# Attention and feed-forward in one kernel: the last 64 rows of unseparated projections as a pair, the output weights in two transfers, and a new timetable

## The chip, the cores and the metric

The kernel runs on one core of a Trainium2 chip. The metric is the time of one execution on the device in microseconds (us), the median of several runs. The engines are TensorE (PE in the profile; PEld is its loading of weights), VectorE (DVE), ScalarE (ACT), GpSimd (POOL) and SyncE (SP), which here does nothing but issue transfers. TensorE writes its results to eight banks of PSUM, from which VectorE and ScalarE read.

## The reference

One layer of a transformer on 2048 tokens of width 576, all in bf16:

```python
# attention, 32 heads of 18, four segments of 512 tokens
q, k, v = (layernorm(x) @ w for w in (wq, wk, wv))          # per head
for s in range(4):
    p = softmax(q_s @ k_s.T * scale + causal_mask)
    a_dot = p @ v_s
    a_mem = phi(q_s) @ M / (phi(q_s) @ z + 1e-6)            # memory of the segments before
    o_s = g * a_mem + (1 - g) * a_dot                        # g = sigmoid(beta), per head
    M += phi(k_s).T @ v_s;  z += sum(phi(k_s))
h = x + concat(o) @ wo
out = h + gelu(layernorm(h) @ w1 + b1) @ w2 + b2             # 576 -> 4608 -> 576
```

## The kernel before, in words

The work is cut into operations (`Op`) of a few instructions each, some 1,900 of them: for each segment s the stages X (layer norm of x and its transposition), P (projections q, k, v), A (scores, exp, mask, values, memory), M (update of the memory), B (output projection, residual, layer norm), C (first matrix of the feed-forward, `F1`) and D (second matrix, `F2`). A tag and a name make a key: `P1Pk` is the first half of the k projection in stage P of segment 1, `P1Rk` its second half, and the index after it is the tile of 128 tokens.

**The order is written out.** `TIMETABLE` gives every operation a rank and an engine: in `"P1Pk": "p 222 159 318 243"` the four tiles' first halves run on TensorE (p) at ranks 222, 159, 318 and 243; a is ScalarE, d VectorE, g GpSimd, s SyncE. `Graph.schedule` takes the operations by rank, gives out the buffers (`Slots`, `Buf.pick`) and keeps an account of the time with a cost for each operation. Each engine issues its own operations in that order, so one that waits holds up everything behind it on its engine. The account steers which buffer is taken and in which form a projection is made; it does not delay anything on the chip. For a transfer it takes `dma = max(dma, op.end) + op.size / 295e3` and then 1.8 us until the data can be used.

**Projections.** A projection multiplies 128 tokens by a 576 x 576 matrix, in two halves of 288 columns that go to two PSUM banks. The 576 rows of the contraction are laid out as five blocks: four of 128 rows and a last one of 64, which is stored twice, once in partitions 0 to 63 for the first half of the columns and once in 64 to 127 for the second, with zeros elsewhere. `proj_pair` has two ways to make it:

- *separated*: `fn_a` (`P`) runs pairs of 64-row matmuls, the lower rows for one bank, the upper rows for the other, side by side in the array: five pairs; `fn_b` (`R`) makes four more pairs with the banks changed over. Between the two a small memset on VectorE or GpSimd (`pass`) keeps them apart.
- *unseparated* (`fused`): where P and R stand next to each other in TensorE's order, ten full-row matmuls of 128 rows run at R's place (L885) and P and `pass` issue nothing. The last block costs a full matmul for each half although half of its rows are zeros.

TensorE works in one tile mode at a time: 128 rows (full), 64-row pairs (`rows64`: separated projections and F1), four 32-row tiles (`rows32`: scores), four 32-column tiles (`cols32`: values). The account charges `SWITCH["pe"]` for each change of mode.

**Transfers.** Nearly all are issued by SyncE (`load`, L663; `flip`, L670, a transfer that transposes; `qkst`, L951). In the first minute these matter here: the loads of x and of the weights q, k, v; the first load of x is followed by a mark (`gate_x`, L743) that has to be made before the third tile of x and the q weights are issued; `dma` 4 is beta (to 32 gates), 5 the output weights (`wt_o`, 720 KB in one transfer), 6 the bias b1, 7 the bias b2. `A0flip` 0 to 7 turn q and k of segment 0, `X1flip`, `X2flip`, `X3flip` the normalized x of the later segments (`xreg<-xnd`), `A1flip` and so on q and k of the later segments into four score buffers (`qk`).

In the lines of the profile L859 is the pair of 64-row matmuls in `rows`, L885 the full-row matmul of `fn_b`, L898 the plain projections of the first two tiles, L802 a transposition on TensorE, L1067 and L1227 the scores, L1098 and L1252 the values, L1198 and L1201 the memory, L1364 and L1401 F1, L1453 F2, L1016 the exp, L677 to L683 the copies out of PSUM.

## Time and profile before

| | |
|---|---|
| median of three runs | 439.85 us (439.02, 439.85, 442.82) |
| span of the profiled execution | 439.3 us |
| TensorE busy | 431.0 us (98%), 5182 matmuls |
| VectorE, ScalarE, GpSimd busy | 288.5, 298.2, 176.5 us |
| transferred | 75.61 MB, mean 172 GB/s |
| packets of the queues named instruction | 56 (q8: 40, q14: 16) |

The profiled execution's own time is its span, 439.3 us, from the first to the last instruction; the runs' times were taken apart from it and lie between 0.3 us below and 3.5 us above. A row of groups reads: line, engine, operation, out<-in, shapes, count, then busy us and mean ns of one, then the idle time before them and who ended it. In the chain of work each piece begins where the one before it ended, so a change of mode in front of it is part of it. A row of busy time by stretch gives for each engine the busy us and the number of instructions.

### The profile page before, as it was taken

To read this page: it belongs to the slowest core of one execution; us is meant where nothing else is said; L and a number is where in the kernel's file an instruction comes from. 1 tells how busy PE (TensorE), PEld (TensorE's weight loads), DVE (VectorE), ACT (ScalarE), POOL (GpSimd) and SP (SyncE) were. 2 spreads that over 40 slices of the span, in tenths; PEclk is the share of its full clock that TensorE was granted. 3 is DMA by queue.
4 is the path that set the end of the run, shared out by engine and by line. 5 is a ranking of instruction groups with operands and counts; after the bars stand their busy time and mean duration, and the time that the engine had idled before them with its cause. 6 is when DMAs were issued, how large, how long until landed. Compare 5 with 4: busy or idle time off the path is not lost.

```text
span 439.3 us, 12412 instructions
## 1 busy us (share of the span) xinstructions
PE 431.0 (98%) x5182; PEld 279.0 (64%) x5182; DVE 288.5 (66%) x641; ACT 298.2 (68%) x325; POOL 176.5 (40%) x328
## 2 busy tenths in 40 slices
PE   8998999999999999999999999999999999999997
PEld 5665677776677676664445766654457785446886
DVE  5898889988997987975698897766776211000002
ACT  5997988999888897788898976657864003465000
POOL 6676866445867644571631462320203001020001
PEclk9999999999999999999999999999999999999999
DMA  7699999989899758973671859506405752450011
GB/s 229 214 209 230 347 262 273 234 274 229 236 235 340 196 157 231 229 157 101 155 185 26 243 152 213 107 18 213 140 25 143 233 131 81 151 175 1 1 58 51
DMA packets 80280, 75.61 MB, mean 172 GB/s; under 512 B 57952, under 2 KB 67424, under 8 KB 80224
## 3 DMA queue, kind: packets, MB, share of 16 engines
q1 hardware_dynamic: 80080, 74.74, 63.9%
q8 instruction: 40, 0.66, 0.7%
q14 instruction: 16, 0.13, 0.1%
q10 hardware_dynamic: 144, 0.09, 0.1%
HBM read 42.30 MB, written 18.87 MB: 139 GB/s over the span
## 4 chain that ended last, share of the span: by engine, by line
PE 89%; DMA 4%; DVE 3%; SPq 1%; POOL 1%; ACT 1%; issue 1%; DVEq 0%; POOLq 0%
PE bank L1453 33%; PE bank L1364 24%; PE bank L859 9%; PE bank L1401 8%; PE bank L1227 4%; PE bank L885 3%; PE bank L1252 3%; DMA xreg<-xnd 2%; DMA x<-in_A_x_dram 2%; PE bank L1201 1%; PE bank L1098 1%; PE bank L1067 1%; SPq L663 1%; SPq L670 1%; PE bank L1198 1%
## 5 line engine op out<-in xcount | busy, mean ns | idle before, releaser
L1016 ACT ACTIVATE pt<-bank 128x1024 bf16<-128x1024 f32 x160 | 155.5, 1021 | 36.7 <-PE bank L1227 26.5
L1453 PEld LDWEIGHTS <-hT 128*128 128x128 bf16 x1188 | 111.3, 98 | 33.4 <-issue 6.6
L1364 PE MATMUL bank<-xreg,w1g 64*128 64x512 bf16 x972 | 107.7, 377 | 0.0
L1364 PEld LDWEIGHTS <-w1g 64*128 64x128 bf16 x972 | 46.2, 94 | 57.2 <-issue 3.0
L1453 PE MATMUL bank<-w,hT 128*128 128x288 bf16 (+2 forms) x594 | 77.8, 283 | 0.0
L1453 PE MATMUL bank<-w_lo,hT 128*128 128x288 bf16 (+2 forms) x594 | 77.6, 283 | 0.0
L1466 DVE TENSOR_TENSOR ot<-bank,hc 128x288 bf16<-128x288 f32 (+2 forms) x33 | 14.1, 444 | 85.1 <-PE bank L1453 79.6
L1241 POOL TENSOR_SCALAR_AFFINE_SELECT pt<-pt 128x512 bf16<-128x512 bf16 x57 | 38.0, 680 | 45.4 <-ACT pt L1016 45.1
L1369 ACT ACTIVATE hT<-bank,b_col 128x512 bf16<-128x512 f32 x36 | 22.1, 690 | 46.4 <-PE bank L1364 46.3
L1439 POOL TENSOR_TENSOR hc<-hc,b_bc 128x576 f32<-128x576 f32 x11 | 14.5, 1333 | 83.6 <-DMA hc<-hd 83.6
L1379 DVE TENSOR_SCALAR hT<-bank,b_col 128x512 bf16<-128x512 f32 x45 | 32.6, 742 | 19.4 <-PE bank L1364 17.3
L1401 PE MATMUL bank<-xreg,w1g 64*128 64x256 bf16 x648 | 38.4, 270 | 0.0
L1401 PEld LDWEIGHTS <-w1g 64*128 64x128 bf16 x648 | 30.5, 94 | 6.6 <-issue 3.2
L1384 ACT ACTIVATE hT<-hT 128x8192 bf16<-128x8192 bf16 (+2 forms) x6 | 31.8, 5320 | 0.1
L859 PE MATMUL bank<-hT,xreg 64*128 64x288 bf16 x414 | 27.7, 283 | 1.7 <-DMA xreg<-xnd 1.7
L885 PE MATMUL bank<-hT,xreg 128*128 128x288 bf16 x210 | 28.4, 287 | 0.3 <-ACT pt L1016 0.2
L1412 DVE TENSOR_TENSOR hT<-bank,b_col 128x512 bf16<-128x512 f32 x33 | 21.4, 681 | 6.3 <-PE bank L1401 5.9
L1377 ACT ACTIVATE hT<-bank,b_col 128x512 bf16<-128x512 f32 x27 | 17.8, 686 | 11.4 <-PE bank L1364 11.0
L859 PEld LDWEIGHTS <-xreg 64*128 64x128 bf16 x414 | 19.6, 94 | 8.3 <-DMA xreg<-xnd 1.9
L1227 PE MATMUL bank<-qk 32*128 32x512 bf16 (+3 forms) x384 | 24.2, 301 | 0.2 <-DVE hT L1379 0.2
L885 PEld LDWEIGHTS <-xreg 128*128 128x128 bf16 x210 | 19.7, 98 | 6.4 <-issue 1.0
L773 POOL TENSOR_TENSOR ln<-ln,mhalf 128x1 f32<-128x1 f32 x32 | 19.5, 610 | 2.7
(122 smaller groups left out, 566.4 us busy)
## 6 DMA issues: line engine op xcount, KB each, us to landing
w1g<-in_B_w_dram SPq DMA_DIRECT2D x41, 576.0 KB, 4.9
qkd<-qk_pad SPq DMA_DIRECT2D x15, 512.0 KB, 4.7
hd<-h SPq DMA_DIRECT2D x16, 288.0 KB, 4.6
hc<-hd SPq DMA_DIRECT2D x16, 288.0 KB, 4.0
w_lo<-in_B_w_dram SPq DMA_DIRECT2D x3, 864.0 KB, 7.2
w<-in_B_w_dram SPq DMA_DIRECT2D x3, 864.0 KB, 8.4
xb<-in_A_x_dram SPq DMA_DIRECT2D x16, 144.0 KB, 4.7
x2d<-xn SPq DMA_DIRECT2D x14, 160.0 KB, 2.8
```

The source lines that it names most:

```text
L859: return nc.tensor.matmul(out=half(hf), lhsT=xTb.t[r, k, ts], rhs=wt[r, hf, k, :], start=start, stop=stop, skip_group_check=True)
L885: nc.tensor.matmul(out=half(hf), lhsT=xTb.t[:, k, ts], rhs=wt[:, hf, k, :], start=(k == 0), stop=(k == KT - 1))
L1016: ops.append(add(prio, {"act": 1.04}, lambda e, j=j: nc.scalar.activation(out=pt.t[:, 2 * j:2 * j + 2, :], in_=st[j].t[:], func=ACT.Exp, s ...
L1227: nc.tensor.matmul(out=st[i // 2].t[:, i % 2, off:off + n_], lhsT=qk[rows, 1, kt * P:(kt + 1) * P], rhs=qk[rows, 0, kt * P:L], start=True, ...
L1241: nc.gpsimd.affine_select(out=blk, in_=blk, pattern=[[0, 4], [1, P]], compare_op=ALU.is_ge, fill=0.0, base=0, channel_multiplier=-1)
L1364: nc.tensor.matmul(out=cc[w].t[:], lhsT=w1.t[rows, k, q, :], rhs=x2T[s].t[rows, k, :], start=(k == 0), stop=(k == ND - 1))
L1369: ready_f[f + w] = [add(pf - 12, {"act": 0.68}, lambda e, f=f, w=w, cc=cc: nc.scalar.activation(out=hT[:, :, f + w, :], in_=cc[w].t[:].rea ...
L1379: nc.vector.tensor_scalar(out=dst, in0=src, scalar1=b, scalar2=None, op0=ALU.add)
L1384: ge = add(2.9, {"act": 0.42 * (f1 - f0) + 0.2}, lambda e, f0=f0, f1=f1: nc.scalar.activation(out=hT[:, :, f0:f1, :], in_=hT[:, :, f0:f1, ...
L1401: nc.tensor.matmul(out=cc[w].t[:, q * 2 * P:(q + 1) * 2 * P], lhsT=w1.t[rows, k, q, :], rhs=x2T[s].t[rows, k, ts], start=(k == 0), stop=(k ...
L1412: nc.vector.tensor_tensor(out=dst, in0=src, in1=b.unsqueeze(2).to_broadcast([P, 2, 2 * P]), op=ALU.add)
L1453: nc.tensor.matmul(out=c.t[:, 0:c1 - c0], lhsT=hT[:, tl // 2, f, (tl % 2) * P:(tl % 2 + 1) * P], rhs=w2_c[ch][:, f - ch * WCH, c0:c1], sta ...
```

## The change

Three things change in the code, and with them the timetable.

1. An unseparated projection can take one of two new forms. With `first`, the 64 rows of the last block go first, as one pair in the two halves of the array, and then four full-row matmuls for each half of the columns; with `last` the pair comes at the end. The form is chosen in `schedule`, where by its account (`TAILED`, and `SWITCH` for each change of mode) it costs less than the plain one.
2. The output weights come in two transfers of 360 KB, issued at two places.
3. The account of transfers in `schedule` counts TensorE's instructions: for each `FETCH` matmuls a fetch of `LAG` us is added to a second clock of the transfers, and a transfer ends with the later of the two clocks plus `LAND`. The sizes and costs that the account uses for many transfers and a few operations are changed (qkst from 560e3 to 342e3, the flips of x2 from 520e3 and 420e3 to 953e3 and 667e3, the beta load from 8e3 to 250e3, gates from 1.7 to 0.73 us, and so on); these numbers alone issue nothing.
4. `TIMETABLE` is new throughout: nearly every rank changes, and some operations change their engine. The rows that the text below speaks of are shown.

```diff
-SWITCH = dict(act=1.35, pe=0.1)
+SWITCH = dict(act=1.35, pe=0.095)
 FUSED = 1.225
+TAILED = 1.103
...
-    "A00st0": "p 96 115",
+    "A00st0": "p 86 108",
...
-    "A0flip": "s 104 112 120 118 180 193 207 287",
+    "A0flip": "s 127 116 140 146 168 182 198 326",
...
-    "A1flip": "s 449 405 534 607 496 636 667 788",
+    "A1flip": "s 411 409 558 591 466 655 475 770",
...
-    "P1Pk": "p 222 159 318 243",
+    "P1Pk": "p 215 161 306 237",
-    "P1Rk": "p 226 165 322 257",
+    "P1Rk": "p 222 164 313 241",
...
-    "X00dma": "s 22 26 32 14",
+    "X00dma": "s 44 49 51 17",
-    "X1dma": "s 63 72 176 161",
-    "X1flip": "s 198",
+    "X1dma": "s 61 70 176 155",
+    "X1flip": "s 228",
-    "X3flip": "s 490 604",
+    "X3flip": "s 491 593",
-    "b1": "d 313",
-    "dma": "s 1 12 13 39 28 195 144 262",
+    "b1": "a 257",
+    "dma": "s 1 15 16 59 55 256 935",
-    "gate": "g 7",
-    "gates": "a56 d79",
+    "gate": "g 12",
+    "gates": "a66 d67",
-    "memset": "d10 g27 g54 d30 a50 a69 a66 a91 g47 g15 g6",
+    "memset": "d7 g27 g8 d11 a125 a48 a58 a28 g9 g29 g4",
-    "tri": "g 82",
+    "tri": "g 10",
+    "wodma": "s 195 81",
...
+MATMULS = dict(F1=18, F2=6, st=7, st0=13, val=16, mem=3, TX=5, TQ=8, T=5, M=16, warm=4, C00F1=36, C01F1=36, A01val=48)
+MATMULS.update({h + nm: 10 if h == "P" else 8 for h in "PR" for nm in "kqvo"})
+FETCH, LAG, LAND = 128, 0.66, 1.95
...
             if op.fused:
                 c = 0.0 if op.mate is not None else FUSED
-            kind = op.mode if e == "pe" else op.table
+                if op.mate is None:
+                    was, then = table.get("pe"), op.next_mode
+                    s = SWITCH["pe"]
+                    plain = FUSED + s * (was != "full") + s * (then != "full")
+                    first = TAILED + s + s * (was != "rows64") + s * (then != "full")
+                    last = TAILED + s + s * (was != "full") + s * (then != "rows64")
+                    if min(first, last) < plain - 1e-9:
+                        op.form = "first" if first <= last else "last"
+                        c = TAILED + s + s * (was != ("rows64" if op.form == "first" else "full"))
+                        table["pe"] = kind = "full" if op.form == "first" else "rows64"
...
+            issued += op.mm if e == "pe" else 0
+            while issued >= fetched:
+                pending.append(t0)
+                fetched += FETCH
...
             if e == "sp":
+                while pending and pending[0] <= op.end:
+                    slow = max(slow, pending.pop(0)) + LAG
                 dma = max(dma, op.end) + op.size / 295e3
-                op.end = dma + 1.8
+                slow = max(slow, op.end) + op.size / 295e3
+                op.end = max(dma, slow) + LAND
...
+                n = KT if b.form is None else KT - 1
+                if b.form == "first":
+                    for w in range(2):
+                        rows(w, w, KT - 1, True, False)
                 for hf in range(2):
-                    for k in range(KT):
-                        nc.tensor.matmul(out=half(hf), lhsT=xTb.t[:, k, ts], rhs=wt[:, hf, k, :], start=(k == 0), stop=(k == KT - 1))
+                    for k in range(n):
+                        nc.tensor.matmul(out=half(hf), lhsT=xTb.t[:, k, ts], rhs=wt[:, hf, k, :], start=(k == 0 and b.form != "first"),
+                                         stop=(k == n - 1 and b.form != "last"), skip_group_check=True)
+                if b.form == "last":
+                    for w in range(2):
+                        rows(w, w, KT - 1, False, True)
...
-        w_ok["o"] = load_w(4, "o", 3, begin)
+        gr.tag = "wo"
+        w_ok["o"] = [load(4, lambda h=h: wts["o"][:, h, :, :].rearrange("p k d -> p (k d)"),
+                          lambda h=h: A_w[3 * P:4 * P, h * KT * HALF:(h + 1) * KT * HALF], 316e3, [xn_ok[0, 0]]) for h in range(2)]
+        gr.tag = ""
```

With the output weights out of the row `dma`, its index 5 is b1 and 6 is b2 in the new timetable. TensorE's ranks of the steps that the text names, before and after: `A1st` 3 at 582 and 585, `P3Pk` 2 at 634 and 640, `D00hc` 0 at 848 and 936.

66 lines of the change are left out of this document (36 added, 30 removed), and 603 rows, old and new, of the table TIMETABLE.

## The prediction

> **What bounds the kernel now.** I read the page first, then the busy time by stretch, then TensorE's waits.
>
> ```profile
> span 439.3 us, 12412 instructions
> PE 431.0 (98%) x5182; PEld 279.0 (64%) x5182; DVE 288.5 (66%) x641; ACT 298.2 (68%) x325; POOL 176.5 (40%) x328
> ```
> ```profile
> 0.00:60.00 60.00, 54.63 (x820) 38.27 (x822) 50.21 (x129) 50.14 (x71) 42.67 (x109) 1.00 0.92 245
> 60.00:366.00 306.00, 305.79 (x3720) 195.86 (x3715) 232.71 (x500) 225.92 (x219) 130.07 (x217) 1.00 0.69 180
> ```
> ```profile
> PE bank L859 <- DMA xreg<-xnd: 1.7, 1, 1.7
> PE bank L692 <- PEq L1609: 0.8, 1, 0.8
> PE bank L939 <- ACT qk_pad L677: 0.5, 1, 0.5
> PE bank L1098 <- DVE pt L1079: 0.4, 1, 0.4
> PE bank L1067 <- DVE MZacc L996: 0.4, 2, 0.2
> PE bank L802 <- DVE xn L788: 0.3, 1, 0.3
> ...
> PE bank L1227 <- DVE hT L1379: 0.2, 1, 0.2
> ```
>
> TensorE is the bound, at full clock. Its idle time is 5.4 us in the first 60 us (60 less 54.63) and 0.2 us in the next 306. The longest waits (all eleven add up to 5.3 us) sit in the first stretch too, where the 16 DMA engines are 92% busy. The rest of the 8.3 us idle is the tail behind the last matmul, which the change leaves as it is. So the change can win in two ways only: fewer matmuls or mode changes, or waits in the first minute of the timetable. It can lose anywhere, because the timetable of every engine is new.
>
> **Fewer matmul slots, more mode changes.** The counts per projection come from these groups, the price of one from two pieces of the chain that follow different neighbours:
>
> ```profile
> L885 PE MATMUL bank<-hT,xreg 128*128 128x288 bf16 x210 | 28.4, 287 | 0.3 <-ACT pt L1016 0.2
> L859 PE MATMUL bank<-hT,xreg 64*128 64x288 bf16 x414 | 27.7, 283 | 1.7 <-DMA xreg<-xnd 1.7
> L859 PE MATMUL bank<-wt_o,oT 64*128 64x288 bf16 x234 | 15.7, 283 | 0.0
> ...
> L885 PE MATMUL bank<-wt_o,oT 128*128 128x288 bf16 x30 | 4.2, 287 | 0.0
> ```
> ```profile
> 85.43 0.33 PE bank L1227 x8
> 85.76 2.56 PE bank L885 x20
> 88.31 0.33 PE bank L1227 x8
> 88.64 7.82 PE bank L859 x126
> ...
> 97.44 0.32 PE bank L1198
> 97.77 2.45 PE bank L885 x20
> ```
>
> A separated projection is 18 matmuls, an unseparated one 10: (414+234)/18 = 36 and (210+30)/10 = 24, together the 60 of the code. Twenty full-row matmuls take 2.45 us behind a full-row matmul (L1198) and 2.56 behind a 32-row score (L1227): 0.1225 us each, 1.225 an unseparated pass, and about 0.1 for a change of tile mode. The seven separated passes (x126, 63 pairs) take 7.82: less the change, 0.122 a pair, so 1.10 for the nine pairs. A tailed pass has one pair and eight full-row matmuls, 9 x 0.1225 = 1.10.
>
> In the new timetable 34 projections have both halves next to each other. By the rule in the scheduler 30 of them get the tail (17 first, 13 last; each stands beside an operation of another mode) and 4 stay plain. So 20 fewer plain passes: 20 x (1.225 - 1.10) = -2.5 us. Reading TensorE's order in both timetables, mode changes rise from 193 to 222, with the one inside each tail: 29 x 0.10 = +2.9 (2.8 at 0.095, the diff's own figure; 3.2 at 0.11). Net **+0.4 us** (0.2 to 0.8). No cover: TensorE is the bound. Ten fewer separated passes also means ten fewer marks (`pass`) on VectorE and GpSimd; no wait of TensorE on them is listed, so nothing.
>
> **The flip that TensorE waits for.** SyncE issues in order:
>
> ```profile
> 30.20 0.59 SPq L663 DMA_DIRECT2D wt_o<-in_A_w_dram  x1
> 30.90 1.25 SPq L670 DMA_TRANSPOSE xreg<-xnd  x1
> 32.75 0.33 SPq L951 DMA_DIRECT2D qkd<-qk_pad  x1
> 33.13 3.79 SPq L670 DMA_TRANSPOSE w_lo<-qkd  x1
> ```
> ```profile
> 30.90 9.12 DMA xreg<-xnd
> ```
> ```profile
> DMA  1000699999990900000000000090000001909939
> ...
> q14 instruction: 1, 0.01, 3.0%
> q8 instruction: 1, 0.02, 1.7%
> ```
>
> The last view is 36 to 40 us in 40 slices. The flip X1flip lands 9.1 us after its issue, and TensorE, ready at 38.4 (40.07 less 1.67), waits. Ahead of the flip stand the 720 KB of output weights. But from slice 13 to 34 (2.2 us) the engines move almost nothing although four transfers are under way; in that time two instruction packets run, 1.7% and 3.0% of 16 x 4 us, or 1.1 and 1.9 us. So half of this wait belongs to the fetches, which come with the count of instructions, not with the order of the transfers.
>
> The new order sends one half of the output weights ahead (behind the load of x, order 81, where DMA has room) and leaves 360 KB at the old place. But it also puts X1flip behind A0flip6, the transposing load at 33.13, whose issue alone held SyncE 3.79 us. TensorE comes to X1flip's first user, P1Pk3, behind the same work. Lower end: the wait goes, -1.7. Upper end: A0flip6's issue again stands 3.79 us, X1flip is issued at 34.6 and needs 9.1, lands at 43.7: a wait of 5.3, or +3.6. The half that left takes about 2 us off (6.4 against 4.4 below), one more flip puts back 1.3 (its usual issue), and the fetch finds X1flip under way again. I take a wait of 1.5: **-0.2**, nearest the row of the wait itself.
>
> **The start.**
>
> ```profile
> 3.28 0.18 POOL L743 CAST mark<-x 1x1 f32<-1x1 bf16 x1 [1.02 <-DMA x<-in_A_x_dram]
> 11.03 0.23 ACT L1507 ACTIVATE g_bc<-beta_bc 128x32 f32<-128x32 bf16 x1 [1.44 <-DMA beta_bc<-in_A_beta_dram]
> ```
> ```profile
> L659 POOL MEMSET qk_pad<- 128x896 bf16 x2 | 1.7, 842 | 0.0
> ...
> L1490 POOL TENSOR_SCALAR_AFFINE_SELECT tri<-tri 128x128 bf16<-128x128 bf16 x1 | 0.3, 293 | 0.1
> L1489 POOL MEMSET tri<- 128x128 bf16 x1 | 0.2, 204 | 0.0
> ```
>
> - The beta load moves behind the third load of x, so x lands earlier and the wait on VectorE's xn (L802, 0.3) goes: **-0.3**.
> - ScalarE's gates exp waits for beta with the q copy queued behind it; the new order has it behind the copy: -0.4 of the 0.5 us wait at L939. Against this, GpSimd now makes one qk_pad memset (0.84), the gmz column and tri (0.5) ahead of the mark that lets SyncE issue the q weights; it was free 1.02 us before, so the mark comes about 0.4 later, and the q weights are used as they land: +0.4. Together **0** (-0.4 to +0.4).
> - The first scores (A00st0) go ahead of a projection, so exp and mask start about half a microsecond earlier; of the waits on masks and banks (L1098, L1067: 1.1 with the smaller ones) I take a third, **-0.4** (0 to -1.1).
>
> **Other moved transfers.**
>
> ```profile
> hT<-in_A_w_dram SPq DMA_DIRECT2D x4, 360.0 KB, 4.4
> ...
> wt_o<-in_A_w_dram SPq DMA_DIRECT2D x1, 720.0 KB, 6.4
> ...
> b_bc<-in_B_b_dram SPq DMA_DIRECT2D x1, 144.0 KB, 6.4
> ...
> xreg<-xnd SPq DMA_TRANSPOSE x5, 6.4
> ...
> ot<-in_B_b_dram SPq DMA_DIRECT2D x1, 9.0 KB, 3.9
> ```
>
> The b1 load comes later and its copy goes from VectorE to ScalarE: in that queue P1's ek and the exps of A02 stand behind a load that takes 3.9 us; cover is the projections B00 and B01, which need no ScalarE, so 0, and up to +3.9 with the cover gone. The b2 load goes from the first minute to just ahead of its first user, the hc of D00; 6.4 us, covered by D00's own F2 groups and six other banks: 0.
>
> In segment 1, X3flip1 now stands behind A1flip3, which waits for a score buffer that the step A1st3 frees. TensorE has 7.4 us of work from there to the flip's user P3Pk2 (three unseparated passes 3.7, one pair of separated ones 2.2, steps and values 1.5); A1flip3's issue 1.3 and the usual 6.4 of such a flip make 7.7: **+0.3** (0 to +3.0, when it takes 9.1 as above). All other weight loads are issued at the same distance or earlier: 0, as only 0.2 us of waits stood there before.
>
> By the Trainium skill ("DMA: Bandwidth & Descriptors", section "Bandwidth"), larger transfers run nearer the peak; its table (0.95 us for 64 KB, 6.15 for 1 MB) gives, as an estimate, 0.6 us fixed for each. By that the split would cost 0.6 us of queue and the sum would be 440.2; the rows above (360 KB 4.4, 720 KB 6.4) show only that two halves in turn would be dearer, not two that overlap. The same page (section "Queues, rings and completion order") says that each DMA engine takes turns between queue rows packet by packet; then a fetch costs one packet's turn, 1.1 us, not the 2.2 seen, and the sum would be 1.1 lower.
>
> **The sum.** +0.4 -0.2 -0.3 +0 -0.4 +0.3 = -0.2 against the span of 439.3: 439.1. The median of the runs, 439.85, is 0.5 above that span, so **439.6 us**.
>
> **The rivals.**
>
> - *The account is right and the first minute closes up.* X1flip's wait goes (-1.7), TQ's (-0.4), xn's (-0.3), the mask waits (-1.1), against +0.4: -3.1, or 436.7. For it: nothing after 60 us waits. Against it: the fetch at 36 us will come again.
> - *SyncE stands at A0flip6* (the other side). X1flip lands at 43.7: +3.6, with +0.4 and -0.7 of the start +3.3: 443.1. It decides where that issue takes more than about 2.5 us. For it: the row with 3.79. Against it: with 360 KB less queued the issue should come nearer the usual 1.3.
> - *X3flip1 is late by the whole 3.0* behind A1flip3: 442.3. It decides above 6.1 us from issue to landing.
> - *The tails do not pay.* Within the forecast: 2.5 won, 2.9 spent, so the change to tails alone is no gain.
>
> **How the numbers follow.** Forecast 0.55 (own range 438 to 441.3), first minute closed 0.17, SyncE at A0flip6 0.16, X3flip1 0.12. The range 436.8 to 443.3 leaves out about 2 in 10. A measurement of this kernel can tell about 1% from no change, 4.4 us. Faster by that needs nearly all of the 5.3 us of waits gone despite the switches: 0.04, out of the second case. Slower needs one of the last two with more than its price, or both: 0.12. Within: 0.84.
>
> **What the profile would show.** L885 with some 280 matmuls (30 x 8 + 4 x 10) and the line of the pairs with 528 (26 x 18 + 30 x 2); TensorE's busy time within 1 us of 431; the wait on xreg<-xnd between 0.5 and 2.5 us; L802 on xn L788 gone, a wait of the q weights new; next to no waits after 60 us apart from X3flip1. I am wrong if a wait above 2 us stands anywhere, or if TensorE's busy time falls by over 1 us.

## The result, and the profile after

The changed kernel takes 441.95 us (median of 20 runs, 440.53 to 444.33) against 440.36 us for the kernel before (20 runs, 438.68 to 443.13): a ratio of **1.0035 [1.0018, 1.0052]**, 1.5 us more. The forecast was 0.2 us less: the time lies in the forecast range, but on the other side of no change. Repeats on other occasions gave 1.0097 [1.0071, 1.0123] and 1.0078 [1.0047, 1.0108]: the first figure is the lowest of three.

The page's first lines for the changed kernel, and its busy time by stretch (busy us and instructions of PE, PEld, DVE, ACT, POOL):

```profile
span 439.7 us, 12220 instructions
PE 430.8 (98%) x5099; PEld 282.9 (64%) x5099; DVE 296.8 (67%) x651; ACT 300.4 (68%) x331; POOL 162.3 (37%) x304
```
```profile
0.00:60.00 60.00, 56.15 (x815) 38.00 (x816) 53.46 (x134) 50.50 (x70) 41.63 (x104) 1.00 0.94 259
60.00:366.00 306.00, 303.97 (x3638) 199.98 (x3636) 237.35 (x505) 227.73 (x226) 118.14 (x198) 1.00 0.67 179
```

The span is 0.4 us longer, but the loss has moved. Of its first 60 us TensorE now idles 3.9 us instead of 5.4; in the next 306 it idles 2.0 us instead of 0.2. VectorE is busy for 8 us more, GpSimd for 14 less. The execution with this profile took 441.45 us; a run's time is its span and about 1.75 us in every run below (1.7 to 1.8).

So a span and a median can't be compared as they stand. With the 1.75 us, the execution from which the kernel before was read counts as a run of about 441.05 us, 0.7 above its kernel's median, while the one above is 0.5 below the median of its own. That is why the two profiles lie 0.4 us apart and the medians 1.6.

The groups of the projections, and TensorE's longest waits (us in total, times, longest):

```profile
L917 PE MATMUL bank<-hT,xreg 128*128 128x288 bf16 x230 | 31.4, 287 | 0.2 <-ACT xreg L707 0.2
L887 PE MATMUL bank<-hT,xreg 64*128 64x288 bf16 x338 | 26.7, 284 | 0.3 <-DVE qk_pad L711 0.2
L887 PE MATMUL bank<-wt_o,oT 64*128 64x288 bf16 x190 | 13.6, 283 | 0.9 <-DVE oT L1317 0.9
...
L917 PE MATMUL bank<-wt_o,oT 128*128 128x288 bf16 x50 | 7.0, 287 | 0.0
```
```profile
PE bank L887 <- DVE oT L1317: 0.9, 1, 0.9
PE bank L720 <- PEq L1648: 0.8, 1, 0.8
PE bank L1288 <- DVE pt L1275: 0.8, 1, 0.8
PE bank L830 <- DVE xn L814: 0.8, 2, 0.5
PE bank L1103 <- DVE qk_pad L711: 0.7, 1, 0.7
PE bank L1103 <- DVE t L1148: 0.6, 1, 0.6
```

(After the change L887 is the pair of 64-row matmuls, L917 the full-row matmul of `fn_b`, L1103 and L1263 the scores, L1134 and L1288 the values, L830 the transposition, L1275 and L1277 the mask on VectorE and GpSimd, L1068 the swap, L1317 the transposition of the attention's output, L1475 hc.) Pairs and full matmuls are 528 and 280, as counted. The wait for the flip `xreg<-xnd` is gone from this execution. Two waits on VectorE are new and lie at 154.6 and 281.8 us: the first and the third row. The trace around the first (start, duration, engine, operation):

```profile
153.20 2.58 POOL L1475 TENSOR_TENSOR hc<-hc,b_bc 128x576 f32<-128x576 f32 x2
153.42 1.20 DVE L1068 COPY o_nat<-o_nat 64x256 bf16<-64x256 bf16 x1
...
154.73 0.71 DVE L1317 STREAM_TRANSPOSE oT<-o_nat 128x512 bf16<-128x512 bf16 x1
...
155.50 1.77 PE L887 MATMUL bank<-wt_o,oT 64*128 64x288 bf16 x26 [0.88 <-DVE oT L1317]
```

The swap, a small copy, takes 1.20 us on VectorE while GpSimd makes the two hc additions of D00, 1.29 us each; it ends 0.1 us after the first of them. Behind it stands the transposition, and behind that TensorE's output projection. `D00hc` was at 848 on VectorE and 941 on GpSimd and is now at 936 and 938 on GpSimd, behind the b2 load, which moved from the first minute to rank 935; the swap `A1swap` 1 went from GpSimd to VectorE. Around the second:

```profile
278.34 2.31 DVE L1307 TENSOR_TENSOR o_nat<-t,t 128x288 bf16<-128x288 f32 x2 [0.80 <-POOL t L1249]
...
278.88 1.47 POOL L1475 TENSOR_TENSOR hc<-hc,b_bc 128x576 f32<-128x576 f32 x1
...
282.14 0.38 DVE L1275 TENSOR_TENSOR pt<-pt,tri 128x512 bf16<-128x512 bf16 x1
...
282.57 1.26 PE L1288 MATMUL bank<-pt,v_aug 128*19 128x512 bf16 x32 [0.80 <-DVE pt L1275]
```

Two additions on VectorE take 2.31 us beside an hc that moved to GpSimd (`D1hc` 2, d1523 to g1520), VectorE falls behind, and the mask for which TensorE waits, `A3mask` 21, stands in VectorE's queue behind them. That mask did not change its engine (d1502, now d1511). The same operations on VectorE in the groups of the kernel before and of the changed one:

```profile
L1271 DVE TENSOR_TENSOR o_nat<-t,t 128x288 bf16<-128x288 f32 x11 | 5.7, 527 | 0.1
...
L1032 DVE COPY o_nat<-o_nat 64x256 bf16<-64x256 bf16 x4 | 1.5, 371 | 0.2
```
```profile
L1307 DVE TENSOR_TENSOR o_nat<-t,t 128x288 bf16<-128x288 f32 x14 | 10.8, 780 | 0.9 <-POOL t L1249 0.8
...
L1068 DVE COPY o_nat<-o_nat 64x256 bf16<-64x256 bf16 x3 | 2.0, 668 | 0.1
```

The mean of one addition rose from 527 to 780 ns, of one copy from 371 to 668, with nothing changed in the operation itself. Both means mix operations that ran while GpSimd was idle with others that ran beside one of its operations: of the fourteen additions in the changed kernel's trace the former take 447 to 460 ns, the latter 0.5 to 1.5 us.

### The profile page after: what moved, and what is told of

Same layout as the page of the kernel before. It is cut to its first block, busy times and chain, and to the rows that moved or that the text cites. A ratio compares the mean times of both kernels' runs of the same rounds, so it can differ in the third digit from the quotient of the medians.

```text
span 439.7 us, 12220 instructions
## 1 busy us (share of the span) xinstructions
PE 430.8 (98%) x5099; PEld 282.9 (64%) x5099; DVE 296.8 (67%) x651; ACT 300.4 (68%) x331; POOL 162.3 (37%) x304
## 4 chain that ended last, share of the span: by engine, by line
PE 85%; DVE 9%; DMA 1%; POOL 1%; issue 1%; ACT 1%; SPq 0%; DVEq 0%; POOLq 0%
PE bank L1489 29%; PE bank L1400 24%; PE bank L887 8%; PE bank L917 7%; PE bank L1437 7%; PE bank L1263 4%; PE bank L1288 3%; DMA beta_bc<-in_A_beta_dram 1%; PE bank L1103 1%; DVE oT L1317 1%; PE bank L1134 1%; DVE pt L1275 1%; PE bank L1237 1%; DVE t L1243 1%; DVE qk_pad L711 1%
## 5 line engine op out<-in xcount | busy, mean ns | idle before, releaser
L1400 PEld LDWEIGHTS <-w1g 64*128 64x128 bf16 x972 | 52.2, 94 | 50.6 <-issue 3.1
L1277 POOL TENSOR_SCALAR_AFFINE_SELECT pt<-pt 128x512 bf16<-128x512 bf16 x44 | 30.8, 711 | 50.1 <-ACT pt L1052 50.0
L1475 POOL TENSOR_TENSOR hc<-hc,b_bc 128x576 f32<-128x576 f32 x11 | 14.7, 1340 | 85.1 <-DMA hc<-hd 85.1
L1415 DVE TENSOR_SCALAR hT<-bank,b_col 128x512 bf16<-128x512 f32 x43 | 30.8, 739 | 10.8 <-PE bank L1400 7.4
L1437 PEld LDWEIGHTS <-w1g 64*128 64x128 bf16 x648 | 30.4, 94 | 6.7 <-issue 3.2
L917 PE MATMUL bank<-hT,xreg 128*128 128x288 bf16 x230 | 31.4, 287 | 0.2 <-ACT xreg L707 0.2
L1275 DVE TENSOR_TENSOR pt<-pt,tri 128x512 bf16<-128x512 bf16 x52 | 22.9, 453 | 7.1 <-ACT pt L1052 7.1
L887 PE MATMUL bank<-hT,xreg 64*128 64x288 bf16 x338 | 26.7, 284 | 0.3 <-DVE qk_pad L711 0.2
L917 PEld LDWEIGHTS <-xreg 128*128 128x128 bf16 x230 | 21.1, 98 | 7.3 <-issue 0.9
L1263 PE MATMUL bank<-qk 32*128 32x512 bf16 (+3 forms) x384 | 24.3, 301 | 0.3
L1448 DVE TENSOR_TENSOR hT<-bank,b_col 128x512 bf16<-128x512 f32 x31 | 20.2, 682 | 4.1 <-PE bank L1437 3.8
L887 PEld LDWEIGHTS <-xreg 64*128 64x128 bf16 x338 | 15.5, 94 | 9.9 <-issue 5.0
```

The source lines that it names most:

```text
L887: return nc.tensor.matmul(out=half(hf), lhsT=xTb.t[r, k, ts], rhs=wt[r, hf, k, :], start=start, stop=stop, skip_group_check=True)
L917: nc.tensor.matmul(out=half(hf), lhsT=xTb.t[:, k, ts], rhs=wt[:, hf, k, :], start=(k == 0 and b.form != "first"), stop=(k == n - 1 and b.f ...
L1263: nc.tensor.matmul(out=st[i // 2].t[:, i % 2, off:off + n_], lhsT=qk[rows, 1, kt * P:(kt + 1) * P], rhs=qk[rows, 0, kt * P:L], start=True, ...
L1275: nc.vector.tensor_tensor(out=blk, in0=blk, in1=tri[:].unsqueeze(1).to_broadcast([P, 4, P]), op=ALU.mult)
L1277: nc.gpsimd.affine_select(out=blk, in_=blk, pattern=[[0, 4], [1, P]], compare_op=ALU.is_ge, fill=0.0, base=0, channel_multiplier=-1)
L1400: nc.tensor.matmul(out=cc[w].t[:], lhsT=w1.t[rows, k, q, :], rhs=x2T[s].t[rows, k, :], start=(k == 0), stop=(k == ND - 1))
```

## The experiments

Three questions: does the loss sit in the tails, in the new order of the first minute, or in the new order behind it; are the two waits on VectorE its cause there; and why does the changed kernel spread more than the one before. Every ratio is to the kernel before on the same chip. "Old order" is the timetable of before under the new code.

### One part at a time

**after_plain**: the changed kernel with every unseparated projection as ten full matmuls; the order, and the account that made it, are kept.

```diff
-                n = KT if b.form is None else KT - 1
-                if b.form == "first":
+                form = None
+                n = KT
+                if form == "first":
...
```

> The new kernel with every unseparated projection made of ten full-row matmuls again; timetable, account and buffers as in the new kernel. Theory ORDER (the loss comes from the new timetable, past the first minute, where TensorE waits for VectorE; the tails pay a little): TensorE's work rises by 30 x 0.1225 = 3.7 us and falls by 24 mode changes x 0.095 = 2.3 us, so +1.4 us over the new kernel: about 443.3 us, 0.6% to 0.7% over the kernel before. Rival SWITCH (the mode change inside a tail costs more than the pair saves): faster than the new kernel, by 1 to 1.5 us, so near 440.5.

443.72 us, 1.0081 [1.0063, 1.0100]. It lies among the three measurements of the changed kernel itself (1.0035 to 1.0097), so the tails' worth in the new order can't be told from it. Its profiled execution has a late first minute with the wait on `xreg<-xnd` back (1.8 us), which no tail can cause.

**old_order**: all the new code, with the ranks of before; the output weights stay split, their first half behind `X1dma` 1.

```diff
-    "P01qkst": "s 144 130",
+    "P01qkst": "s 117 95",
...
-    "A1swap": "g904 d908",
+    "A1swap": "d895 g899",
...
-    "wodma": "s 195 81",
+    "wodma": "s 195 72.5",
```

> The old timetable (ranks and engines) under the new code: tails where the rule gives them (19 of 24 unseparated projections), output weights in two transfers (the first half behind the load X1dma 1, the second at the old place), new account. Theory ORDER: no loss; 19 tails win 0.7 us by the prices of the rows and the flip's wait of 1.7 us shrinks, so 0 to 2 us under the kernel before, 438.5 to 440.4. Rival SWITCH: 19/30 of the loss, so about 1 us over the kernel before, 441.4. Rival SPLIT (two transfers are dearer than one, or the account's other choice of buffers does harm): also over the kernel before, by 1 to 1.5 us, with waits on xreg<-xnd or wt_o.

439.41 us, 0.9984 [0.9970, 0.9998], the only kernel of the study whose interval lies below 1 (that of its repeat, at the end, does not). So neither the tails, 19 in this order, nor the split costs time that can be seen: the loss is in the order.

**new_then_old** and **old_then_new**: the new order up to rank 390 with the old behind it, and the reverse (390 is about where stage P of segment 1 ends). The ranks are numbered through; these rows show the seam:

```diff
 new_then_old
-    "A1swap": "g904 d908",
+    "A1swap": "d896 g900",
-    "D00hc": "g 936 938",
+    "D00hc": "d849 g942",
 old_then_new
-    "A0flip": "s 127 116 140 146 168 182 198 326",
+    "A0flip": "s 105 113 121 119 181 194 208 288",
-    "P01qkst": "s 144 130",
+    "P01qkst": "s 118 96",
```

> The new code with a mixed timetable: the new order for all operations up to rank 390 (about the first 60 us), the old order for the rest. Theory ORDER: keeps the 1.5 us that the first minute won in the profile and loses none of the 1.8 us behind it: 1 to 2 us under the kernel before, 438.4 to 439.4. Rival SWITCH or SPLIT: over the kernel before, 441 to 442.

> The new code with the other mixture: the old order up to rank 390, the new order for the rest. Theory ORDER: keeps the 1.8 us of waits past the first minute and the old waits of the first: 442 to 443.5, with TensorE waiting 1.5 us or more past 60 us, on VectorE's results. Rival SWITCH or SPLIT: like the new kernel, 441.5 to 442, and like new_then_old.

new_then_old: 440.36 us, 1.0003 [0.9990, 1.0016], where 438.4 to 439.4 was expected. old_then_new: 441.94 us, 1.0044 [1.0027, 1.0061], with both waits on VectorE at their places. Against old_order on the same chip, the new order behind rank 390 costs 0.0060 (2.6 us), and the new first minute costs 0.0019 (0.8 us), though it was there that the forecast had its gain. The first of these is far outside the noise, the second is as large as its own uncertainty (0.0019).

**old_plain** and **old_one_wo**: old_order without the tails (the edit of after_plain), and old_order with the output weights in one transfer of 720 KB at the old place.

```diff
-    "wodma": "s 195 72.5",
+    "wodma": "s 195",
...
-        w_ok["o"] = [load(4, lambda h=h: wts["o"][:, h, :, :].rearrange("p k d -> p (k d)"),
-                          lambda h=h: A_w[3 * P:4 * P, h * KT * HALF:(h + 1) * KT * HALF], 316e3, [xn_ok[0, 0]]) for h in range(2)]
+        w_ok["o"] = load_w(4, "o", 3, begin)
```

> As old_order (old timetable, new code, output weights in two transfers) but with every unseparated projection made of ten full-row matmuls. If tails pay by the rows: 19 tails are 0.7 us, so 440.1 against 439.4; if they pay as measured in after_plain (2.0 us for 30): 1.2 us, 440.6. Rival SPLIT (the gain of old_order comes from the two transfers and the flip's wait that goes): stays at 439.4 to 439.7.

> As old_order (old timetable, tails) but with the output weights in one transfer of 720 KB at the old place. If the split takes the flip's wait away: the wait on xreg<-xnd of 1.7 us is back in the profile and the time is 0.5 to 1.7 us over old_order, 439.9 to 441. If the split does nothing: 439.4, and the gain of old_order is all from the tails.

old_plain: 440.01 us, 0.9995 [0.9978, 1.0011]: the tails win about 0.5 us (0.0011) in the old order, inside the noise but of the size that the prices give (0.7); against the repeat of old_order it is 0.0002. old_one_wo: 440.44 us, 1.0011 [0.9992, 1.0031]: the split is worth about 1.2 us (0.0027, with an uncertainty of 0.0024), and 0.8 (0.0018) against the repeat. TensorE's first wait in old_one_wo:

```profile
PE bank L887 <- DMA xreg<-xnd: 1.8, 1, 1.8
```

With the split, this wait stands in none of seven profiles: old_order, old_plain, old_then_new, and below old_new_moved, new_start, old_gate_late and old_order_again. Without it, in the old order, it stands in two of three: here and in the first profile of the kernel before, but not in its second, below. In six of the seven another wait of TensorE has come up at 47 to 49 us (0.2 to 1.4 us), which none of the three has. In old_order:

```profile
46.65 0.82 DVE L785 BATCH_NORM_STATS2 ln<-x 128x6 f32<-128x288 bf16 x2 [1.28 <-DMA x<-in_A_x_dram]
...
48.35 1.77 PE L887 MATMUL bank<-hT,xreg 64*128 64x288 bf16 x26 [0.81 <-DVE b_col L1566]
```

VectorE has waited for a load of x, and TensorE then waits for VectorE: part of what the split wins is given back 10 us later.

### The two waits on VectorE

**new_hc_held**: the changed kernel with the two hc additions of D00 held back until the last transposition of A1, by a semaphore.

```diff
+                    def hc_fn(e, hc=hc, held=s == 0 and tl < 2):
+                        i = VEC[e].tensor_tensor(out=hc.t[:], in0=hc.t[:], in1=b2_bc[:], op=ALU.add)
+                        if held:
+                            tc.add_manual_dep(i.ins, flipped[1, 4].ins.name, SYNC, reason="after the last transposition of A1")
+                        return i
...
```

> The new kernel; only the two additions of the bias b2 (hc of D00, on GpSimd) are made to wait for the last transposition of A1 (oT 4), so that they don't run beside VectorE's swap. Theory PORT (VectorE's swap takes 1.20 us instead of some 0.4 because GpSimd's hc runs at the same time, and so oT 4 and TensorE's B1Po are late): swap 0.5 us or less, TensorE's wait of 0.9 us on oT falls to 0.2 or less, time 0.7 to 0.9 us under the new kernel, 441.1. Rival QUEUE (VectorE simply has too much queued ahead of oT): the swap may shorten, the wait stays at 0.5 us or more, time as the new kernel, 441.6 to 442.

The trace at the same place:

```profile
155.03 0.22 DVE L1069 COPY o_nat<-o_nat 64x256 bf16<-64x256 bf16 x1
155.36 0.71 DVE L1318 STREAM_TRANSPOSE oT<-o_nat 128x512 bf16<-128x512 bf16 x1
```

The same swap on the same engine takes 0.22 us with GpSimd's hc out of the way, against 1.20, and TensorE's wait there is gone. The other profiles with the new order behind rank 390 and the swap on VectorE show the same, with nothing held back. In four of them (the changed kernel, old_then_new, new_gate_early and new_store_mid) hc began 0.03 to 0.32 us before the swap, the swap took 1.20 to 1.32 us, and TensorE waited 0.9 to 1.0. In three (after_plain, new_again and new_third) hc began 0.12 to 0.56 us after it, the swap took 0.22, and there was no wait. In new_third:

```profile
157.14 0.22 DVE L1068 COPY o_nat<-o_nat 64x256 bf16<-64x256 bf16 x1
157.26 2.52 POOL L1475 TENSOR_TENSOR hc<-hc,b_bc 128x576 f32<-128x576 f32 x2 [0.42 <-DMA b_bc<-in_B_b_dram]
```

There hc had waited for the b2 load to land. So the mechanism is shown at this place, and in the changed kernel whether the wait stands is settled by which comes first, the swap or the landing of the b2 load. By the Trainium skill ("SBUF — State Buffer", section "Who interferes with whom") VectorE and GpSimd share a port pair, and a copy in a two-port mode or an operation with two SBUF inputs blocks against GpSimd until the other is done. The trace agrees: the swap ended 0.1 us after the first addition (154.62; the addition 153.20 and 1.29), 1.20 us long instead of 0.22. The time did not follow (441.1 was expected): 442.75 us, 1.0067 [1.0044, 1.0091], within the spread of the changed kernel. Matched with the changed kernel's first trace, this execution won 1.0 us at 155 us, but had lost 1.4 at 95 us, in part waiting on other copies of VectorE (L711), and it kept the mask wait of 0.8.

**new_two_moved** puts the swap back on GpSimd in the changed kernel, and the mask `A3mask` 21 too (which was on VectorE in the kernel before); **old_new_moved** does the same in old_then_new, where the first minute is the old one.

```diff
-    "A1swap": "g904 d908",
+    "A1swap": "g 904 908",
 in the row "A3mask", index 21
-d1511
+g1511
```

> The new kernel with two operations changed from VectorE to GpSimd at their ranks: the second swap of A1 and the mask A3mask 21, ahead of the two waits of 0.9 and 0.8 us that came back in two profiles. Theory TWO WAITS (the loss past the first minute is these two): both gone, 1.5 to 1.7 us under the new kernel, 440.2 to 440.5, level with the kernel before. Rival SPREAD (the loss is spread over many small waits that vary from run to run): at most 0.8 us under the new kernel, 441.2 or more.

> The kernel of old_then_new (old order to rank 390, new order behind it; 1.0044 against the kernel before) with the swap A1swap 1 and the mask A3mask 21 put back on GpSimd. TWO WAITS: the waits of 0.9 and 0.8 us are what the rest of the new order loses beside TensorE's work; both go and the ratio falls by 0.0039 to about 1.0005. OTHER: what stands behind the waits takes the time up again, and the ratio stays above 1.003. Between the two, about 1.002, if one of the waits is given back.

new_two_moved: 441.13 us, 1.0026 [1.0005, 1.0047], between the two expectations, and hardly below the changed kernel's first figure (1.0035), though below its repeats (1.0097 and 1.0078). old_new_moved: 440.13 us, 1.0008 [0.9992, 1.0023], against 1.0044 for old_then_new: **-0.0036, 1.6 us**, where the two waits were 0.9 + 0.8. Busy time of TensorE (after the length of the stretch) in old_then_new, then in old_new_moved:

```profile
120.00:180.00 60.00, 59.02 (x811) 1.00 0.73 219
240.00:300.00 60.00, 59.20 (x610) 1.00 0.51 134
```
```profile
120.00:180.00 60.00, 59.89 (x836) 1.00 0.76 220
240.00:300.00 60.00, 60.00 (x618) 1.00 0.53 139
```

Both waits are real losses, and two engine letters take them away. At the second place the letter does two things. The mask leaves VectorE's queue, and on GpSimd it stands ahead of `D1hc` 2, which so comes later and no longer runs beside the two additions (old_new_moved):

```profile
278.25 0.83 DVE L1307 TENSOR_TENSOR o_nat<-t,t 128x288 bf16<-128x288 f32 x2 [0.80 <-POOL t L1249]
...
281.46 1.28 POOL L1475 TENSOR_TENSOR hc<-hc,b_bc 128x576 f32<-128x576 f32 x1
```

The additions take 0.83 us instead of 2.31, that is 1.5 us less for a wait of 0.8. By these numbers hc beside VectorE would be enough to make this wait too; which of the two effects took it away was not tried by itself.

What remains against old_order, 0.0024 or 1.1 us (0.0015 against its repeat), is of the size that the forecast's prices give for ten more unseparated passes: 1.2 (see the prediction's account below). Against the repeat it is inside the noise, and no run tries it by itself.

### The unsteady first minute

**new_start** has the new order up to rank 75 only; **before_again** is the kernel before with a second profile; **new_again** is the changed kernel, a second time.

```diff
 new_start
-    "A0flip": "s 127 116 140 146 168 182 198 326",
+    "A0flip": "s 106 114 122 120 182 195 209 288",
-    "P01qkst": "s 144 130",
+    "P01qkst": "s 119 97",
     "gate": "g 12",
```

> The changed kernel with the new order up to rank 75 only (loads of x and q weights, memsets, gate, beta, gates, first projections) and the old order behind it. To be set beside old_order (0.9984) and beside the new order up to rank 390 (1.0003). START GAINS (the forecast's step, -0.3 us): ratio 0.9975 to 0.998 and the wait on xn smaller. START LOSES (the mark and the q weights come later): 0.9995 or more, with a wait on hT or qk_pad in the first 15 us; then the 0.8 us between the two kernels are in the start. If it comes out as 0.9984, they lie between rank 75 and 390.

> The kernel before, one more profile. If the wait on the flip X1flip (1.67 us at 38.4 us) belongs to the order of the transfers, it is there again with 1.2 to 2.2 us; if it belongs to the fetch that happened to fall on it in the profiled execution, it is below 1 or gone. TensorE busy 430.5 to 431.5 us, and next to no waits after 60 us.

> The changed kernel as it is, a second time, to see how its first minute differs from one execution to the next and to have it on the same chip as the two below. STEADY (the first minute has the same waits in each execution): TensorE busy 56.1 us (plus or minus 0.3) of the first 60, ratio 1.0035. UNSTEADY (its waits on transfers come and go): another amount, between 54.5 and 56.8, and the two waits of 0.8 to 0.9 us at 154.6 and 282.6 us at their places again, since they need no transfer; ratio within 1.001 to 1.006.

new_start: 439.50 us, 0.9999 [0.9985, 1.0013]. By its ratio this is START LOSES (0.9995 or more), but the wait that should go with it is not in its profile, and the interval overlaps that of old_order: the new start does not gain the 0.3 us of the forecast, and it does not clearly lose. before_again: one run of 439.28 us, span 437.6, and its longest waits:

```profile
PE bank L692 <- PEq L1609: 0.8, 1, 0.8
PE bank L802 <- DVE xn L786: 0.7, 2, 0.4
PE bank L1098 <- DVE pt L1079: 0.4, 1, 0.4
```

The flip wait of 1.7 us, on which much of the forecast's middle part rested, is not there. It belonged to the profiled execution. new_again: 444.11 us, 1.0097 [1.0071, 1.0123], with waits on the q weights (0.9), on a flip of q and k (1.0) and on `xreg<-xnd` (1.0), and TensorE busy for 54.35 of the first 60 us. So its first minute is UNSTEADY, but two things came out otherwise than expected: the ratio lies above the range (1.001 to 1.006), and of the two waits on VectorE only the second is there. The first does need a transfer, the b2 load.

To see where executions part, each matmul of one trace is matched with the same of another, and the difference of their starts is followed. The means over each stretch, in us:

| trace less trace | 14 us | 20-40 | 40-60 | 120-140 | 160-180 | end |
|---|---|---|---|---|---|---|
| before_again - before | -0.4 | -0.4 | -2.2 | -1.9 | -1.9 | -1.8 |
| new_again - changed kernel | 1.0 | 1.6 | 3.1 | 4.1 | 3.1 | 3.1 |
| new_third - changed kernel | 0.5 | 1.6 | 3.2 | 3.7 | 2.7 | 2.7 |
| new_two_moved - changed kernel | 0.5 | 0.9 | 2.0 | 1.9 | 0.9 | 0.0 |
| old_new_moved - old_then_new | 0.6 | 0.6 | 0.6 | 0.7 | -0.4 | -1.3 |
| old_gate_late - old_order | 0.3 | 0.4 | 0.7 | 1.3 | 1.3 | 1.3 |

(14 stands for 14 to 15 us; new_third is the changed kernel once more, below.) In the new first minute a start that is 0.5 to 1.0 us late has become 2 to 3 us late by 45 us; in the old one 0.9 at 13 us has become 0.6 at 14 and stays 0.6. The table shows a second place too: between 90 and 106 us new_again and new_third lost another 0.5 to 0.8 us against the changed kernel's first trace, as did new_hc_held, new_gate_early and new_store_mid (0.6 to 1.4). No experiment takes that up. It also shows what became of the two waits in new_two_moved: its execution was 2.0 us late at 60 us, won 1.0 at 155 and 0.9 at 282, and ended where the changed kernel's had.

The way from one to the other, in SyncE's queue of new_third and then of old_new_moved. The `qkd` rows are the stores of q and k, the `qk` rows the flips that read them back:

```profile
13.14 0.35 SPq L987 DMA_DIRECT2D qkd<-qk_pad  x1
...
18.18 2.60 SPq L698 DMA_TRANSPOSE qk<-qkd  x2
20.88 0.52 SPq L987 DMA_DIRECT2D qkd<-qk_pad  x1
...
23.03 0.53 SPq L987 DMA_DIRECT2D qkd<-qk_pad  x1
23.61 1.62 SPq L698 DMA_TRANSPOSE qk<-qkd  x1
```
```profile
13.16 0.35 SPq L987 DMA_DIRECT2D qkd<-qk_pad  x1
...
17.10 0.34 SPq L987 DMA_DIRECT2D qkd<-qk_pad  x1
17.75 2.63 SPq L698 DMA_TRANSPOSE qk<-qkd  x2
21.12 0.34 SPq L987 DMA_DIRECT2D qkd<-qk_pad  x1
21.52 2.73 SPq L698 DMA_TRANSPOSE qk<-qkd  x2
```

The first store is issued at the same time in both. In the old order the second store goes out while the first is under way; in the new one it stands behind the first two flips, which wait for the first store to land, and goes out 3.8 us later. The third store then goes out 1.9 us later, and new_third's chain of waits (start, us, what) runs from there to the flip of x:

```profile
13.14 5.03 DMA qkd<-qk_pad
...
18.27 0.65 ACT qk_pad L707
...
23.03 5.26 DMA qkd<-qk_pad
...
35.18 4.68 DMA xreg<-xnd
```

Between the first store and the third this chain runs through ScalarE, not through the second store: at 18.27 us ScalarE goes on when the first store has landed (its idle time before it, 0.24 us, ended with `qkd<-qk_pad`), and the data of the third are there at 23.03. And the first store itself took 5.0 us to land, against 3.6 in the changed kernel's first trace. So the second store's place in the queue is one candidate among others. The forecast did name a queue behind A0flip6; this one is 15 us earlier (18.18 against 33.13), behind `A0flip` 1 and 0.

**new_gate_early**, **old_gate_late**, **new_store_mid**, **new_gate_moved** try this chain: the mark ahead of the q weights earlier in the new order, later in the old one, the second store between the two flips, and the early mark together with the two engine letters of new_two_moved.

```diff
 new_gate_early, new_gate_moved
-    "gate": "g 12",
+    "gate": "g 4.5",
 old_gate_late, against old_order
-    "memset": "d10 g27 g54 d30 a50 a69 a66 a91 g47 g15 g6",
+    "memset": "d10 g6.8 g54 d30 a50 a69 a66 a91 g6.6 g6.3 g6",
 new_store_mid
-    "P01qkst": "s 144 130",
+    "P01qkst": "s 144 121",
```

> The changed kernel with one rank changed: the mark that lets SyncE issue the q weights stands right behind the first memset of GpSimd again, as in the order before (issue about 3.35 us instead of 3.75 for the third load of x, so the q weights 0.4 earlier). AMPLIFIED (in the new order a q weight that lands late makes the first store of q and k late, the two flips behind it, the second store behind them and so the last flips of segment 0: 0.8 to 1.0 us at 10 us became 2.0 to 3.1 us at 45 us in two executions): the median falls by 1 to 2 us against the changed kernel's 442 to 444, to a ratio of 1.000 to 1.003, and the profile has no wait on hT above 0.5 us. SEPARATE (the waits of the first minute do not hang on the q weights): less than 0.5 us, ratio 1.0035 to 1.009 as in the two measurements of the changed kernel.

> The kernel of old_order with three memsets of GpSimd put ahead of the mark (0.94, 0.1 and 0.8 us, into a gap of 0.88), so that the q weights are issued about 0.9 us later than before. The old order of SyncE has the second store of q and k ahead of the first flips. DAMPED (AMPLIFIED is a property of the new order of stores and flips): a wait on hT of 0.8 to 1.2 us near 9 us, but no more than 0.8 us of it left at 45 us; ratio 0.999 to 1.001 against 0.9984. If lateness grows in the old order too: 2 us and more, ratio 1.003 or above.

> The changed kernel with the second store of q and k (P01qkst 1, rank 130) between the first two flips instead of behind both. In the two late executions it had its data 1.4 to 2.0 us before SyncE came to it. If the stand at SyncE is what amplifies: the median falls by 0.5 to 1.3 us (ratio 1.001 to 1.005). If it is not, or if the second flip is now the one that comes late: no change or slower, 1.0035 to 1.010.

> The changed kernel with the early mark and with the swap A1swap 1 and the mask A3mask 21 back on GpSimd, so with both losses taken away: the two waits on VectorE past the first minute (-1.6 us) and the late q weights. Against new_two_moved (1.0026): AMPLIFIED gives 0.998 to 1.000, an order as good as the kernel before or better by what the forecast gave to the first minute; SEPARATE gives 1.002 to 1.003.

- old_gate_late: 439.85 us, 0.9994 [0.9974, 1.0014]. TensorE waited for the q weights (0.6 us), was 0.9 us late at 10 us and 0.3 at 14: damped, as expected, and by the ratio 0.4 us against old_order. The 1.3 us at the end of that execution came in later, at 48 and 70 us.
- new_gate_early: 443.56 us, 1.0073 [1.0049, 1.0098]. A miss: the profiled first minute was on time, but the time did not fall. It is a weak test, as the q weights were issued only 0.17 us earlier (3.96 us instead of 4.13) where 0.4 was expected. That execution lost 0.7 us at 95 us, at scores that follow the copies of VectorE, and kept both waits.
- new_store_mid: 442.93 us, 1.0051 [1.0029, 1.0072], inside the spread of the changed kernel; it tells nothing apart. The part of the chain that runs through ScalarE it leaves as it is.
- new_gate_moved: 442.13 us, 1.0038 [1.0019, 1.0057], where 0.998 to 1.000 was expected. Its profiled execution had neither late start nor either wait and took 439.70 us, but that was the shortest of its 12 runs (to 443.34).

So AMPLIFIED is seen in three traces and not found by its remedies. What sets off the late start is open: issued at 4.13 and 4.12 us, the third transfer of weights landed at 8.39 us in the changed kernel's first trace and at 9.94 in new_again, far more than the 0.17 us by which the mark was moved.

**old_order_again** and **new_third**, unchanged copies of old_order and of the changed kernel, side by side:

> The kernel of old_order (old order, with the new forms of projection, the output weights in two transfers and the new account) a second time, beside the changed kernel on the same chip. If the steps add up (split -1.2, tails -0.5, something given back): ratio 0.9970 to 0.9998 again. If the first measurement was chance: 1.000 or above.

> The changed kernel a third time, on the same chip as old_order_again. The sum of the parts says 1.0061: 0.9984 for old_order, +0.0060 for the new order behind rank 390 (0.0036 of it the two waits), +0.0018 for the new order up to rank 390. So far it was measured with 1.0035 and 1.0097; expected between the two, 1.004 to 1.008, and the distance to old_order_again 0.005 to 0.010. If the parts do not add up: a distance below 0.004.

439.50 us, 0.9993 [0.9976, 1.0011], and 442.67 us, 1.0078 [1.0047, 1.0108]: a distance of 0.0085, 3.7 us by the ratios and 3.2 by the medians, inside what the parts gave (0.005 to 0.010). So the new timetable is what costs; with its interval round 1, old_order's gain over the kernel before is not certain.

## Why the prediction was wrong

The place of the forecast was about right (439.6 against 441.95 us), the sign was not: the sum said -0.2 against the profiled span, the measurement +1.5 against the median. That the place came out so near is partly luck: of the two repeats of the changed kernel one, 444.11 us, lies outside the forecast range (to 443.3). The basis was off too. The terms were read from an execution that was itself 0.7 us slower than the median of its kernel, with a wait of 1.7 us that the next one did not have, and were then added to the median of three runs. Point by point:

- **TensorE's work, +0.4: right as far as the runs can tell.** 280 full matmuls and 528 paired, as counted, and 29 more changes of tile mode (205 to 234 in the traces). The busy time, 430.8 against 431.0 us, does not test it, as it was 432.3 and 433.0 in the two later traces of the changed kernel and 430.4 in before_again. By the same prices the tails take 0.7 off the old order, and the new order, with 34 unseparated projections instead of 24, puts 1.2 back: together +0.5. Measured: about -0.5 (old_plain to old_order) and +1.1 (old_order to old_new_moved), the first inside the noise, the second at its edge. So the prices are borne out in sign and size, but not proved: by them the tails do pay a little in the old order, against the rival, and what doesn't pay is making ten more projections unseparated.
- **The flip, -0.2: the direction was right, the size wrong, and the basis one execution.** In the old order the split takes the wait away and is worth 0.8 to 1.2 us, at the edge of the noise, with part of the wait back 10 us later. The wait of 1.7 was in one of the two profiles of the kernel before. In the new order it is absent from the first trace and stands with 0.4 to 1.0 us in new_again and new_third. SyncE did not stand at A0flip6 ahead of it in a way that cost 3.6: in new_third that issue took 2.94 us, and the wait was 0.4.
- **The start, -0.3, 0 and -0.4: wrong in sign.** The wait on xn behind the beta load is gone (L788, now L816), but the other wait on xn (L786, now L814) is 0.8 instead of 0.3, and those on L1103 (`t` 0.6, `qk_pad` 0.7) took the place of the mask waits, so that, the flip aside, the profiled first minute won nothing; over many runs the new first minute costs 0.8 us (new_then_old against old_order) and up to 1.3 (new_two_moved and new_gate_moved, 1.0026 and 1.0038, against old_new_moved, 1.0008), of which only the last is clear of the noise. The wait on the q weights came as named, in two of the three traces of the changed kernel.
- **X3flip1, +0.3: wrong, nothing.** No such wait is in the list.
- **The moves past the first minute, 0: the step that failed.** The prediction put hc at nothing, "covered by D00's own F2 groups and six other banks", the other weight loads at "0, as only 0.2 us of waits stood there before", and gave the operations that change their engine no term at all, though it says itself that the change "can lose anywhere, because the timetable of every engine is new". The cover holds for hc's own user. But hc, moved with its load from rank 848 to 936, ran on GpSimd beside a swap on VectorE, and the swap was held up for 1.0 us. And another hc, which had gone from VectorE to GpSimd, ran beside two additions on VectorE, which took 2.31 us instead of 0.83, with a mask behind them for which TensorE waited. Two waits of 0.9 and 0.8 us, 1.6 by the runs; the whole new order behind rank 390 costs 0.0051 to 0.0060 (2.2 to 2.6 us). That nothing waited before was a property of the old order, not of the stretch: there too a swap took 0.82 us beside an addition on GpSimd, and TensorE waited for none of it. Some 170 operations changed their engine, and neither they nor an operation's duration beside the other engine were costed; it was the transfers that were followed. The signs of being wrong that the prediction named, a wait above 2 us or busy time down by 1 us, did not come; two waits of under 1 us past the first minute were enough.

The sum with the terms measured: old_order -0.0016 and -0.0007 (its two measurements), the new order behind rank 390 +0.0060, the new first minute +0.0018 to +0.0030. Together 1.006 to 1.008, where the changed kernel was measured at 1.0035, 1.0097 and 1.0078. Why the first of these, on record as the result, is the lowest is open, as is the cause of the late starts and of the losses between 90 and 106 us.

## What to carry to other kernels

A timetable that is replaced whole has to be costed engine by engine, not only transfer by transfer: list every operation that changes its engine, and look for what runs beside it on VectorE and GpSimd, with durations from the rows of each pairing. A wait seen in one execution is not a wait of the kernel; before a forecast rests on one, ask whether what it depends on, here the landing of a transfer, has room to vary. Whether a store that feeds a chain of transfers does better ahead of those that wait for the chain's first link, the runs do not show. And a span is compared with spans, a median with medians.

## What the runs showed of the hardware

- A copy of 64 x 256 bf16 on VectorE took 0.22 us, and 1.20 us beside an f32 addition of 128 x 576 on GpSimd. Where the copy began 0.12 us before the addition (new_third) it took 0.22. Additions of 128 x 288 had a mean of 527 ns in one order and 780 ns in another; two of them took 0.83 us with GpSimd idle and 2.31 beside such an addition.
- A transfer of 360 KB, issued at 4.13 and 4.12 us in two executions of one program, landed after 4.3 and 5.8 us.
- Two transfers of 360 KB in place of one of 720 KB took a wait of 1.8 us off the flip behind them, one half of them having left the crowded stretch; 0.0018 to 0.0027 of the time, at the edge of the noise.
- In new_again and new_third TensorE was 3 us late at 45 us, and the wait of 0.9 us on VectorE at 155 us was not there: the b2 load landed 0.05 to 0.5 us after the swap had begun, where in the changed kernel's first trace it had landed 0.3 us before. A loss in one place can take away a wait in another, so waits read from one trace do not simply add.
